# Setting a row of ones earlier and putting five zero matmuls ahead of it, in a fused RWKV-6 and SwiGLU kernel

## The chip, the cores and the metric

The kernel runs on one core of a Trainium2 chip. The core has four compute engines that run unsynchronized: TensorE (PE in the profile; its weight loads are listed as PEld), VectorE (DVE), ScalarE (ACT) and GpSimd (POOL). SyncE (SP) issues most of the transfers. The metric is the device time of one execution in microseconds; several runs are given by their median.

## The reference

Two layers follow each other. The first is a linear recurrence per batch and head with a decaying state, and u is a bonus weight for the current position:

```python
batch, n_heads, seq, head_dim = (4, 8, 768, 48)
for t in range(S):
    cur = einsum('bhd,bhe->bhde', u[None] * kt, vt)
    y[:, :, t] = einsum('bhd,bhde->bhe', rt, state + cur)
    state = wt[:, :, :, None] * state + einsum('bhd,bhe->bhde', kt, vt)
```

Its result, as 3072 rows of 384, goes through a normalization by the root mean square and a gated feed-forward layer of width 1536, whose three weight matrices are w_gate, w_val and w_out:

```python
rms = np.sqrt(np.mean(x * x, axis=-1, keepdims=True) + 1e-06)
xn = x / rms * rms_g
g = xn @ w_gate
return (g * sigmoid(g) * (xn @ w_val)) @ w_out
```

All inputs and the output are float32. The kernel computes most products in bfloat16.

## The kernel before, in words

The sequence is cut into six blocks of 128 positions (n from 0 to 5), and each block has four batches (j from 0 to 3). A tile (n, j) holds 128 positions in the partitions and 8 heads x 48 = 384 columns. For each tile the recurrence is put in its chunked form: the logarithm of w (ln, on ScalarE), its cumulative sums by matmuls with triangular masks (cs_mm), their exponentials (exp_r, exp_k), the products with r and k (r_mul and k_mul), transposes of these (rk_pe on TensorE and rk_tr, a copy out of PSUM), the scores (q_mm), their masking, the new state (st_mm, st_new) and the output (y_mm, x_add). The bonus term r * u * k is done apart: bonus_mul on GpSimd multiplies r by k and then by u_bc, bonus_sum adds up on VectorE, bonus_v multiplies by v. Then come the normalization and the feed-forward part (gate_mm, val_mm, silu, h_mul, o_mm), which take most of TensorE's time.

Every engine takes its instructions in order, and the order is written out by hand: the text ORDER lists all steps as name.n.j, and the loop at the end of the kernel issues them one by one. Transfers of r, k, v and w are issued by SyncE in that order, and it begins with load_r.0.0, load_w.0.0, u_mm.0.0, ln.0.0, load_v.0.0, load_k.0.0 and cs_mm.0.0:2.

A number behind a colon in ORDER asks for zero matmuls ahead of a step's own. They are issued in psum() (L238 and L240), when the step takes its PSUM bank: each multiplies the 128 x 128 tile zero by itself, three times side by side, 384 columns wide, into the bank that the step is about to use, with start and stop set. Their results are overwritten. The list before has such numbers at many steps up to some 38 us, the first of them the 2 of cs_mm.0.0. PSUM has three rings of banks: a and b with two banks each, and q with four (u, v, x, z).

Ahead of the steps stand the constants. VectorE sets zero first (L293), then small columns, the padding of lw and rk, and the state st (L327). GpSimd makes the identity (masks.py:197 and 199), the masks mask_lt (L297, L298) and mask_nle (L303, L304), the mask mw of the first two blocks' cumulative sums (L330 to L335), and then the row of ones (L338) and a small copy (L340).

The row of ones serves one purpose: u arrives as a single row of 384 numbers in the first partition of u_bc, and u_mm (L372) spreads it over the 128 partitions as a float32 matmul of ones_row with that row, into bank u of ring q. u_out (L375, VectorE) copies the result into u_bc, where bonus_mul (L466) reads it. The row u and the gain of the normalization are fetched by two small transfers that ScalarE issues (L288, L289).

Of the kernel before, what the change touches and what calls it, by code (L numbers as in the profile page):

```python
# [9 lines left out]
FP32 = mybir.dt.float32  # L10
# [12 lines left out]


ORDER = """
load_r.0.0 load_w.0.0 u_mm.0.0 ln.0.0 load_v.0.0 load_k.0.0 cs_mm.0.0:2 load_r.1.0 load_w.0.1 u_out.0.0 load_k.1.0
load_k.0.1 load_w.0.3 load_v.0.1 exp_r.0.0 exp_k.0.0 r_mul.0.0 cast_v.0.0 load_r.0.1 bonus_mul.0.0 load_k.1.1
bonus_sum.0.0 bonus_v.0.0 k_mul.0.0 cs_mm.1.0 load_r.1.1 load_v.1.1 load_v.1.0 load_w.0.2 rk_pe.0.0:2 rk_tr.0.0
exp_r.1.0 w_tot.1.0 w_tot.0.0 st_mm.0.0 r_mul.1.0 st_new.0.0 q_mm.0.0:4 load_k.0.3 load_r.0.3 load_r.0.2 load_k.0.2
# [100 lines left out]
def kernel(  # L130
# [13 lines left out]
    nc = tc.nc  # L144
# [16 lines left out]
    const = ctx.enter_context(tc.tile_pool(name="const", bufs=1))  # L161
# [131 lines left out]
    nc.vector.memset(zero, 0.0)  # L293
    ident = const.tile([128, 128], BF16)
    make_identity(nc, ident)
    mask_lt = const.tile([128, 128], BF16)
    nc.gpsimd.memset(mask_lt, 0.0)  # L297
    nc.gpsimd.affine_select(  # L298
# [35 lines left out]
    )  # L334
    nc.gpsimd.memset(mw[0:PD, 1], 0.0)  # L335

    ones_row = const.tile([1, 128], FP32)
    nc.gpsimd.memset(ones_row, 1.0)  # L338
    i3 = small.tile([KC, KC], FP32)
    nc.gpsimd.tensor_copy(out=i3, in_=ident[0:KC, 0:KC])  # L340
    wo_sb = persist.tile([128, FC, DM], BF16)
# [372 lines left out]
```

## Time and profile before

| | us |
|---|---|
| median of three runs | 205.89 |
| lowest and highest of them | 205.2 and 206.86 |
| the profiled execution, its own time | 203.96 |
| its span, from the first to the last instruction | 202.2 |
| TensorE busy with matmuls in it | 191.3 |
| VectorE, ScalarE and GpSimd busy | 157.5, 135.0 and 124.4 |

The profile is of one execution. A line of its timeline gives the start and the duration in microseconds, the engine, the line of the kernel, the operation, the tile written and the tiles read, their shapes, and how many alike were merged in one row; a bracket gives the idle time of the engine ahead of it and what ended that. The duration of a merged row reaches from the first start to the last end. Matmuls overlap, so their pace is read from the distance between starts. A row of the table by stage gives for each engine the busy time and, in brackets, how many instructions ran.

### The profile page before, as it was taken

How to read it: one execution, taken by the hardware profiler on the slowest of the kernel's cores; microseconds unless marked ns; L12 is line 12 of the kernel's file. 1: busy time of each engine (PE TensorE's matmuls, PEld its weight loads, DVE VectorE, ACT ScalarE, POOL GpSimd, SP SyncE). 2: the span in 40 equal slices, each digit the busy share in tenths (PEclk: the TensorE clock that was granted, in tenths of full speed). 3: DMA queues.
4: the chain of work that ended last, by engine and by line, in shares of the span. 5: the costliest groups of instructions: out<-in, count | busy, mean ns of one | idle time of the engine just before them, and what ended most of it. 6: DMA issues, size and time to landing. Idle time of an engine off the chain costs nothing.

```text
span 202.2 us, 4604 instructions
## 1 busy us (share of the span) xinstructions
PE 191.3 (95%) x1677; PEld 121.9 (60%) x1694; DVE 157.5 (78%) x307; ACT 135.0 (67%) x278; POOL 124.4 (62%) x178
## 2 busy tenths in 40 slices
PE   1999799999999999999999998999999999999993
PEld 0566485565568998865556664656555555555562
DVE  6489789799989799997999998988989782225711
ACT  2637885779699657898678985899676683335310
POOL 6488959175769962689858556988699554200000
PEclk9999999999999999999999999999999999999999
DMA  6999999999999998989899999995464013030132
GB/s 144 231 234 207 212 208 202 195 179 208 206 184 225 160 212 191 210 185 188 199 176 215 237 188 203 183 190 108 134 179 104 0 23 99 0 117 0 63 115 99
DMA packets 121567, 32.42 MB, mean 160 GB/s; under 512 B 116420, under 2 KB 120392, under 8 KB 121544
## 3 DMA queue, kind: packets, MB, share of 16 engines
q1 hardware_dynamic: 119504, 28.58, 66.6%
q0 software_dynamic: 2032, 3.54, 9.9%
q8 instruction: 13, 0.21, 0.4%
q14 instruction: 10, 0.08, 0.1%
q10 hardware_dynamic: 8, 0.00, 0.0%
HBM read 25.96 MB, written 4.72 MB: 152 GB/s over the span
## 4 chain that ended last, share of the span: by engine, by line
PE 65%; ACT 3%; DMA 2%; DVE 2%; issue 1%; SPq 0%; DVEq 0%; ACTq 0%
PE ps_av L617 7%; PE ps_bu L617 7%; PE ps_au L617 7%; PE ps_bv L617 6%; PE ps_qx L660 6%; PE ps_qv L660 6%; PE ps_qu L660 5%; PE ps_qz L660 4%; PE ps_au L622 2%; PE ps_bu L622 2%; DMA rkT<-rk 2%; PE ps_av L622 2%; PE ps_bv L622 2%; ACT L249 1%; PE ps_au L419 1%; PE ps_qv L500 1%
## 5 line engine op out<-in xcount | busy, mean ns | idle before, releaser
L660 PEld LDWEIGHTS <-ht 128*128 128x128 bf16 x300 | 28.1, 98 | 17.5 <-DVE ht L646 1.0
L251 ACT ACTIVATE sg<-ps_av 128x512 bf16<-128x512 f32 x36 | 21.5, 597 | 22.8 <-PE ps_av L617 18.0
L646 DVE TENSOR_TENSOR ht<-ps_bv,sg 128x512 bf16<-128x512 f32 x29 | 19.9, 687 | 13.9 <-PE ps_bv L617 12.9
L251 ACT ACTIVATE sg<-ps_au 128x512 bf16<-128x512 f32 x36 | 21.5, 596 | 11.5 <-PE ps_au L617 7.7
L617 PEld LDWEIGHTS <-wg_sb 128*128 128x128 bf16 x180 | 19.2, 114 | 15.9 <-issue 0.6
L617 PEld LDWEIGHTS <-wv_sb 128*128 128x128 bf16 x180 | 19.2, 114 | 15.7 <-issue 0.5
L465 POOL TENSOR_TENSOR ruk<-rt,kt 128x384 f32<-128x384 f32 x24 | 24.0, 1001 | 3.7 <-DMA kt<-in_k_dram 2.8
L475 POOL TENSOR_TENSOR ydiag<-vt,diag 128x384 f32<-128x384 f32 x24 | 20.4, 859 | 9.4 <-DVE diag L470 9.1
L617 PE MATMUL ps_av<-xnt,wg_sb 128*128 128x512 bf16 x88 | 25.0, 381 | 0.3
L466 POOL TENSOR_TENSOR ruk<-ruk,u_bc 128x384 f32<-128x384 f32 x24 | 24.0, 1001 | 1.9
L617 PE MATMUL ps_bu<-xnt,wv_sb 128*128 128x512 bf16 x86 | 24.8, 380 | 0.4
L646 DVE TENSOR_TENSOR ht<-ps_bu,sg 128x512 bf16<-128x512 f32 x31 | 21.3, 686 | 4.8 <-PE ps_bu L617 3.1
L617 PE MATMUL ps_au<-xnt,wg_sb 128*128 128x512 bf16 x87 | 23.6, 380 | 0.1
L617 PE MATMUL ps_bv<-xnt,wv_sb 128*128 128x512 bf16 x82 | 23.2, 380 | 0.2
L459 POOL TENSOR_TENSOR rk<-kt,ek 128x384 bf16<-128x384 f32 x16 | 15.9, 1001 | 9.7 <-ACT ek L251 5.9
L249 ACT ACT_TABLE_LOAD x14 | 18.0, 1283 | 1.9 <-PEq L698 1.6
L660 PE MATMUL ps_qx<-wo_sb,ht 128*128 128x384 bf16 x96 | 17.1, 326 | 0.2 <-DVE ht L646 0.2
L558 ACT ACTIVATE junk<-xb 128x384 bf16<-128x384 f32 x24 | 12.5, 522 | 6.3 <-DVE xb L553 6.2
L571 ACT ACTIVATE xn<-xb,rstd 128x384 bf16<-128x384 f32 x24 | 14.2, 609 | 0.6 <-POOL rstd L567 0.5
L470 DVE TENSOR_REDUCE diag<-ruk 128x8 f32<-128x384 f32 x24 | 13.1, 544 | 1.9 <-POOL ruk L466 1.9
L660 PE MATMUL ps_qv<-wo_sb,ht 128*128 128x384 bf16 (+1 forms) x84 | 13.8, 314 | 0.0
L251 ACT ACTIVATE lw<-wt 128x384 bf16<-128x384 f32 (+1 forms) x20 | 11.6, 583 | 2.8 <-DMA wt<-in_w_dram 2.7
(170 smaller groups left out, 408.2 us busy)
## 6 DMA issues: line engine op xcount, KB each, us to landing
rt<-in_r_dram SPq DMA_DIRECT2D x24, 192.0 KB, 4.0
vt<-in_v_dram SPq DMA_DIRECT2D x24, 192.0 KB, 3.9
kt<-in_k_dram SPq DMA_DIRECT2D x24, 192.0 KB, 3.9
out_dram<-ob SPq DMA_DIRECT2D x23, 192.0 KB, 2.2
wt<-in_w_dram SPq DMA_DIRECT2D x16, 192.0 KB, 3.7
wt<-in_w_dram SPq DMA_DIRECT2D x4, 384.0 KB, 4.3
wo_sb<-in_moe_w_out_dram POOLq DMA_DIRECT2D x3, 384.0 KB, 7.3
wg_sb<-in_moe_w_gate_dram POOLq DMA_DIRECT2D x1, 768.0 KB, 9.2
```

The costliest lines, as they stand in the source:

```text
L249: nc.scalar.preload_act_table_set(table_name)
L251: return nc.scalar.activation(**kw).ins
L459: eng.tensor_tensor(out=rk[:, n % 2, j, 1, :, 0:D], in0=inp["k", n, j], in1=bank["cs_k", n, j][:, 0:DM].rearrange("p (h d) -> p h d", h=H) ...
L465: nc.gpsimd.tensor_tensor(out=ruk[n, j], in0=inp["r", n, j], in1=inp["k", n, j], op=ALU.mult)
L466: nc.gpsimd.tensor_tensor(out=ruk[n, j], in0=ruk[n, j], in1=u_bc, op=ALU.mult)
L470: nc.vector.tensor_reduce(out=diag[n, j].rearrange("p h o -> p (h o)"), in_=ruk[n, j], axis=mybir.AxisListType.X, op=ALU.add)
L475: nc.gpsimd.tensor_tensor(out=ydiag[n, j], in0=inp["v", n, j], in1=diag[n, j].to_broadcast([128, H, D]), op=ALU.mult)
L571: nc.scalar.activation(out=xn, in_=xb[n, j], func=AF.Copy, scale=rstd[n, j][:, 1:2])
L617: nc.tensor.matmul(ps, lhsT=units(ws, c, f), rhs=x[:, c, :], start=(c == 0), stop=(c == KC - 1))
L622: nc.tensor.matmul(ps[:, i * TS // 2:(i + 1) * TS // 2], lhsT=units(ws, c, f + i), rhs=x[:, c, cols], start=(i == 0 and c == 0), stop=(i = ...
L646: nc.vector.tensor_tensor(out=ht[n][:, f, :], in0=v, in1=sg, op=ALU.mult)
L660: nc.tensor.matmul(ps[:, cols], lhsT=ht[n][:, f, b * L:(b + 1) * L], rhs=wo_sb[:, f, cols], start=(f == 0), stop=(f == FC - 1))
```

## The change

The memset of ones_row moves up on GpSimd from behind mw to directly behind the identity, ahead of both masks. In ORDER, u_mm.0.0 becomes u_mm.0.0:5, so five zero matmuls of 384 columns go into u's bank ahead of u's own. Nothing else in the order of any engine changes: VectorE, ScalarE and SyncE issue the same instructions in the same order, and the PSUM banks are the same. On TensorE the five zero matmuls and their five weight loads are its first work; the row of u's matmul follows, and behind it the two zero matmuls of cs_mm.0.0 as before.

```diff
 ORDER = """
-load_r.0.0 load_w.0.0 u_mm.0.0 ln.0.0 load_v.0.0 load_k.0.0 cs_mm.0.0:2 load_r.1.0 load_w.0.1 u_out.0.0 load_k.1.0
+load_r.0.0 load_w.0.0 u_mm.0.0:5 ln.0.0 load_v.0.0 load_k.0.0 cs_mm.0.0:2 load_r.1.0 load_w.0.1 u_out.0.0 load_k.1.0
...
     ident = const.tile([128, 128], BF16)
     make_identity(nc, ident)
+    ones_row = const.tile([1, 128], FP32)
+    nc.gpsimd.memset(ones_row, 1.0)
     mask_lt = const.tile([128, 128], BF16)
...
     nc.gpsimd.memset(mw[0:PD, 1], 0.0)
 
-    ones_row = const.tile([1, 128], FP32)
-    nc.gpsimd.memset(ones_row, 1.0)
     i3 = small.tile([KC, KC], FP32)
```

## The prediction

> **What bounds the kernel now.** I read the busy times first, then the chain of waits, then the opening fifteen microseconds engine by engine, because everything that the change touches ends before the first real matmul at 6.35 us.
>
> ```profile
> span 202.2 us, 4604 instructions
> PE 191.3 (95%) x1677; PEld 121.9 (60%) x1694; DVE 157.5 (78%) x307; ACT 135.0 (67%) x278; POOL 124.4 (62%) x178
> ...
> PE 65%; ACT 3%; DMA 2%; DVE 2%; issue 1%; SPq 0%; DVEq 0%; ACTq 0%
> ```
>
> TensorE is busy for 95% of the span, and it carries nearly all of the chain that ended last. What TensorE loses at the start is therefore lost for good, if the later stages have no slack to take it up. A table by stage tells where it loses:
>
> ```profile
> core 0: us, PE busy (x) PEld busy (x) DVE busy (x) ACT busy (x) POOL busy (x), PEclk, DMA share, GB/s
> 0.00:4.16 4.16, 0.00 (x0) 0.00 (x0) 2.62 (x10) 1.28 (x1) 3.22 (x15) 1.00 0.50 115
> 4.16:6.35 2.19, 2.19 (x5) 0.77 (x5) 0.94 (x2) 0.84 (x1) 0.09 (x1) 1.00 1.12 238
> 6.35:10.20 3.85, 3.85 (x34) 2.48 (x33) 1.61 (x4) 2.38 (x5) 2.37 (x3) 1.00 1.08 238
> 10.20:14.10 3.90, 3.44 (x48) 2.21 (x48) 3.16 (x9) 1.49 (x4) 3.40 (x4) 1.00 1.14 250
> 14.10:24.70 10.60, 9.27 (x122) 6.20 (x123) 9.38 (x19) 7.57 (x18) 9.27 (x12) 1.00 1.09 207
> 24.70:34.00 9.30, 9.25 (x107) 6.44 (x109) 8.09 (x19) 6.09 (x14) 7.12 (x9) 1.00 1.16 205
> ```
>
> TensorE idles for 4.16 us, is then busy without a break to 10.20, loses 0.46 us and 1.33 us in the next two stages, and has next to no gap after 24.7. The transfers run at their full share from 4.16 on. So the opening is a race between the loads and the first head of the chain, and TensorE's matmuls there run at half pace, as these rows of its timeline (start, duration, operation, count) show:
>
> ```profile
> 4.16 1.64 PE L372 MATMUL ps_qu<-u_bc,ones_row 1*128 1x384 f32 x2 [4.16 <-POOL ones_row L338]
> 5.74 0.82 PE L240 MATMUL ps_au<-zero 128*128 128x384 bf16 x2
> 6.35 0.85 PE L404 MATMUL ps_au<-lw,mw 128*128 128x384 bf16 x2
> 6.99 0.40 PE L408 MATMUL ps_au<-mw,lw 128*128 128x1 bf16 x8
> ...
> 9.34 0.84 PE L238 MATMUL ps_qv<-ident,zero 128*128 128x128 bf16 x6
> 9.98 0.70 PE L482 MATMUL ps_qv<-ident,rk 128*128 128x128 bf16 x8
> 10.52 0.33 PE L528 MATMUL ps_qx<-vb,rk 128*128 128x96 bf16 x4
> 10.69 0.81 PE L240 MATMUL ps_qz<-zero 128*128 128x384 bf16 x4
> ...
> 12.34 0.48 PE L411 MATMUL ps_bu<-lw,mw 128*128 128x384 bf16 x2
> 12.66 0.61 PE L482 MATMUL ps_qv<-ident,rk 128*128 128x128 bf16 x8
> ```
>
> Two 384-column matmuls take 6.99 - 6.35 = 0.64 us, 0.32 us each, at the start, and 12.66 - 12.34 = 0.32 us, 0.16 us each, later. Six 128-column transposes from 9.34 take 0.64 us, 107 ns each; the next eight take 10.52 - 9.98 = 0.54 us, which is two at 107 ns and six at about 54 ns. So the clock doubles at about 9.98 + 2 x 0.107 = 10.2 us, which is 6.0 us after TensorE's first matmul. (The PEclk column says 1.00 from the start; it does not know the state before its first record, so I go by the spacing.)
>
> **The change part by part.** First, the row of ones. It moves on GpSimd ahead of the two masks and mw. It depends on nothing but GpSimd's order:
>
> ```profile
> 1.07 0.29 POOL masks.py:199 TENSOR_SCALAR_AFFINE_SELECT ident<-ident 128x128 bf16<-128x128 bf16 x1
> 1.31 0.20 POOL L297 MEMSET mask_lt<- 128x128 bf16 x1
> ...
> 3.66 0.31 POOL L335 MEMSET mw<- 64x260 bf16 x1
> 3.91 0.20 POOL L338 MEMSET ones_row<- 1x128 f32 x1
> ```
>
> It would start where mask_lt starts, at 1.31, and be done at about 1.51 instead of 4.11. The masks and mw each come 0.20 us later, mw at about 3.97 + 0.20 = 4.17; no DMA is issued between them, and SP's and ScalarE's queues keep their order. The cover: mw is first needed by the matmul at 6.35, so there are over 1.8 us in hand. Cost nothing.
>
> Second, the row u itself. Its transfer is issued by ScalarE and moves 1.5 KB; the two packets of its queue between 1.6 and 1.8 us are the row and its completion mark:
>
> ```profile
> DMA packets 2, 0.00 MB, mean 8 GB/s; under 512 B 1, under 2 KB 2, under 8 KB 2
> q10 hardware_dynamic: 2, 0.00, 2.2%
> ```
>
> So u is there by 1.8 us, and the only thing that held u's matmul until 4.16 was the row of ones.
>
> Third, the five zero matmuls. They need only the zero tile, and they stand ahead of u's matmul on TensorE:
>
> ```profile
> 0.88 0.11 DVE L293 MEMSET zero<- 128x64 uint32 x1 [0.88 <-PEq L698]
> ```
>
> With the 0.05 us that passed between the end of the memset of ones (4.11) and the matmul behind it (4.16), they start at about 0.99 + 0.05 = 1.05 (rounded) and take 5 x 0.32 = 1.60 us, to 2.65. By then ones and u are there. u's matmul takes 5.74 - 4.16 = 1.58 us, to 4.23, and the two zero matmuls that were there before take 6.35 - 5.74 = 0.61 us, to 4.84. Then TensorE waits, for the next matmul needs ScalarE's logarithm:
>
> ```profile
> 5.42 0.84 ACT L251 ACTIVATE lw<-wt 128x768 bf16<-128x768 f32 x1 [2.50 <-DMA wt<-in_w_dram]
> 7.42 0.48 ACT L251 ACTIVATE ps_au<-ps_au 128x388 f32<-128x388 f32 x1 [1.16 <-PE ps_au L408]
> ```
>
> The logarithm waits for w's load, which nothing in the change hastens, and ends at 6.26. With an estimated 0.07 us for the hand-over (a little over the 0.05 us between GpSimd's memset and the matmul behind it) the first real matmul starts at 6.33 instead of 6.35. So u's matmul 1.5 us earlier buys 0.02 us: when it stood late it was just not late enough to hold anything. A new hole of 6.33 - 4.84 = 1.49 us stands where TensorE was busy.
>
> u's broadcast is ready earlier too. Its copy waits on VectorE behind the memset of st, and is done near 5.2 instead of 6.4. Who needs it:
>
> ```profile
> 3.25 1.34 DVE L327 MEMSET st<- 128x1536 uint32 x1 [0.27 <-issue]
> 5.84 0.56 DVE L375 COPY u_bc<-ps_qu 128x384 f32<-128x384 f32 x1 [1.25 <-PE ps_qu L372]
> 7.08 1.00 POOL L465 TENSOR_TENSOR ruk<-rt,kt 128x384 f32<-128x384 f32 x1 [2.84 <-DMA kt<-in_k_dram]
> 8.16 1.00 POOL L466 TENSOR_TENSOR ruk<-ruk,u_bc 128x384 f32<-128x384 f32 x1
> 7.93 0.56 DVE L453 TENSOR_TENSOR rk<-rt,ps_au 128x384 bf16<-128x384 f32 x1 [1.54 <-ACT ps_au L251]
> 9.19 0.55 DVE L470 TENSOR_REDUCE diag<-ruk 128x8 f32<-128x384 f32 x1 [0.70 <-POOL ruk L466]
> 9.66 0.54 DVE L459 TENSOR_TENSOR rk<-kt,ps_bu 128x384 bf16<-128x384 f32 x1
> 10.72 0.69 DVE L489 COPY rkT<-ps_qv 128x1024 bf16<-128x1024 bf16 x1 [0.52 <-PE ps_qv L482]
> ```
>
> GpSimd reads u_bc at 8.16, behind its product at 7.08, which waits for k's load. So that gain is worth nothing either.
>
> Fourth, the clock. This is where the change can act, and these same rows price it. If TensorE ran at full pace from 6.33, the cumulative sums of the first head would come earlier by half of 1.0 us; but VectorE takes the k product in order, behind the sum that waits for GpSimd, which waited for k's load: 7.08 + 1.00 + 0.08 + 1.00 = 9.16, then 9.19, then 9.66 to 10.20. The four transposes that need it start after 10.20 whatever the clock was before, and by then the clock is at full pace in this execution. What is left is the start of the copy at 10.72, which could come 0.03 us earlier. The bounds: the stretch from 6.35 to 10.2 holds 3.85 us of matmul at half pace, so an earlier clock can be worth at most half, 1.92 us, and at least nothing. I take 0.03, since the rows show the wait that hides the rest.
>
> The sum is 0.00 + 0.02 + 0.03, about 0.05 us less than the profiled execution. That execution took 203.96 us (span 202.2 and 1.8 around it), 1.93 us less than the median of 205.89 of the three runs, which themselves spread from 205.2 to 206.86. So the forecast on the scale of the median is 205.89 - 0.05, 205.8 us: no change that a measurement can tell. About 1%, 2.06 us, is what a measurement of this kernel can tell from none.
>
> [...]
>
> **The rivals.** A, faster: the clock rises early and something that I take as hidden is not. For it: counting the same 6.0 us of work from 1.05, hole included or not, puts the rise at 7.1 to 8.5 us. Against it: GpSimd's chain to 9.16. Its price goes to the bound above, 203.96 - 1.92 = 202.0 in this execution, 204.0 on the median. It would pass 1% only where executions without a profile rise later than 10.2 now.
>
> B, slower: the hole of 1.49 us undoes the first stretch, and the count of 6.0 us starts anew at 6.33, so that the clock rises at 12.3. For it: before, TensorE has no hole at all between 4.16 and the rise, so nothing in this trace shows a rise behind a broken stretch. Against it: a hole of 0.46 us ahead of 14.05 and the 1.33 us of idle time between 14.10 and 24.70 did not slow the matmuls again. The price: between 10.2 and 12.3 four transposes take 0.05 us more each, and the four zero matmuls at 10.69 take 0.32 instead of 0.16 each: 0.20 + 0.64 = 0.84 us, all ahead of the next head's sums and of VectorE's copy behind them, which waited for TensorE before:
>
> ```profile
> 13.30 0.69 DVE L489 COPY rkT<-ps_qv 128x1024 bf16<-128x1024 bf16 x1 [0.22 <-PE ps_qv L482]
> ```
>
> That gives 206.7. It decides once the rise is later than about 10.7, where the zero matmuls begin; it passes 1% once the clock stays low to about 15 us (2 x 2.06 behind 10.7, and the 0.46 us gap used up), and at 17 us it would give 205.9 + (17 - 10.7) / 2 - 0.46 = 208.6.
>
> [...]
>
> C: the change doesn't do what it says, because the zero matmuls do not count for the clock or TensorE starts late. Then the rise stays at 10.2, and 205.9 results; by the profile this differs from the forecast in the trace only, not in the time.
>
> **How the numbers follow.** The forecast with C, where the rise comes anywhere up to about 11 us and costs or brings under 0.3 us, has 0.52. A has 0.18, of which 0.08 beyond 1%. B has 0.22, of which 0.11 beyond 1%. What I have not named, the spread of runs included, has 0.08, half on each side. So faster has 0.12, slower 0.15 and the same 0.73. The range runs from 204.2, near A's bound, to 207.8, past B at 12.3 and short of its far end; some 0.09 lies below it and 0.11 above.
>
> **What would show it.** In the profile of the changed kernel: five zero matmuls at 1.05 to 2.65, u's matmul at 2.65 released by nothing late, a hole from 4.84 to 6.33 with the logarithm's end as its releaser, the first sum at 6.33, the k product on VectorE still at 9.66 and the copy at 10.72. The spacing of the transposes and zero matmuls between 9 and 13 us tells where the clock rose. I am wrong if VectorE's copies at 10.72 and 13.30 move by more than 0.3 us either way, or if w's and k's loads land at other times.

## The result and the profile after

The changed kernel is slower by half a percent: 206.08 us, median of 22 runs (204.81 to 207.55), against 205.06 us for the kernel before (median of 22, 203.73 to 206.86). The ratio is 1.0048, with a 95% interval from 1.0025 to 1.0070. The forecast was no visible change, 205.8. The profiled execution took 205.05 us (span 203.3), 1.1 us more than that of before. Single executions of either kernel spread over more than the difference, so one pair of profiles can't tell why. A ratio here leaves out executions more than 1.5% above the fastest of their kernel, and two of the profiles below, those of the kernels that the last table calls fill behind and tiny zeros, are of such executions.

The opening came out as worked out. TensorE's timeline of the changed kernel (start, duration, operation, count, and in the bracket the idle time and what ended it):

```profile
1.04 1.78 PE L240 MATMUL ps_qu<-zero 128*128 128x384 bf16 x5 [1.04 <-DVE half_of L311]
2.75 1.64 PE L372 MATMUL ps_qu<-u_bc,ones_row 1*128 1x384 f32 x2
4.33 0.82 PE L240 MATMUL ps_au<-zero 128*128 128x384 bf16 x2
6.13 0.80 PE L404 MATMUL ps_au<-lw,mw 128*128 128x384 bf16 x2 [0.98 <-ACT lw L251]
...
9.71 1.15 PE L482 MATMUL ps_qv<-ident,rk 128*128 128x128 bf16 x8
...
10.98 1.14 PE L240 MATMUL ps_qz<-zero 128*128 128x384 bf16 x4
12.05 0.23 PE L500 MATMUL ps_qz<-rkT 48*128 48x128 bf16 x1
```

The zeros, u's matmul and the hole that the logarithm ends are where the prediction has them; the bracket counts the hole from the end of the last zero matmul and gives 0.98 us. The first sum starts at 6.13, earlier than 6.33, because w's load let the logarithm begin 0.18 us earlier in this execution (5.24 against 5.42). The transposes at 9.71 are all at half pace (eight in 0.94 us, up to the next start at 10.65; eight from 13.24 take 0.44 us), and the trace's clock record begins at 11.63 us. So the clock rose 1.5 us later than in the profile before, which is rival B in a mild form. VectorE's rows answer to those of before:

```profile
9.65 0.54 DVE L459 TENSOR_TENSOR rk<-kt,ps_bu 128x384 bf16<-128x384 f32 x1
10.90 0.69 DVE L489 COPY rkT<-ps_qv 128x1024 bf16<-128x1024 bf16 x1 [0.70 <-PE ps_qv L482]
13.88 0.69 DVE L489 COPY rkT<-ps_qv 128x1024 bf16<-128x1024 bf16 x1 [0.62 <-PE ps_qv L482]
```

The k product is at 9.65 (9.66 before), and the copies are 0.18 and 0.58 us later. But what an opening loses need not last. To see what does, I set the n-th copy, sum or elementwise operation of VectorE beside the same one of the kernel before, whose order is the same. The table gives how much later it starts (us), at the time that it had before:

| profile of | clock rose | 14.6 | 21.2 | 91.2 | 109.1 | 148.6 | 152.6 | 199.0 |
|---|---|---|---|---|---|---|---|---|
| the change | 11.63 | +0.52 | +0.58 | +0.58 | +0.48 | +0.39 | +1.18 | +1.03 |
| the change, second profile | 9.57 | -0.10 | -0.50 | +0.24 | +0.85 | +0.93 | +1.87 | +1.72 |

The second profile comes from an experiment below. Its opening is faster than that of before, and it is still slower in the end. What both have in common is a jump of 0.8 to 0.9 us between 148.6 and 152.6, far from anything that the change touches. TensorE's timeline of the changed kernel has it there:

```profile
150.78 0.81 PE L617 MATMUL ps_au<-xnt,wg_sb 128*128 128x512 bf16 x3
152.30 0.23 PE L500 MATMUL ps_qz<-rkT 48*128 48x128 bf16 x1 [0.71 <-DMA rkT<-rk]
```

In the profile before, the same matmul follows with a much shorter wait:

```profile
150.39 0.81 PE L617 MATMUL ps_au<-xnt,wg_sb 128*128 128x512 bf16 x3
151.13 0.23 PE L500 MATMUL ps_qz<-rkT 48*128 48x128 bf16 x1
```

These scores need two transposed tiles of the last block, which SyncE transposes by DMA (line 487) at 147.2 and 148.6 us. The answer for that line gives the time from issue to landing, for the four transposes between 146.4 and 156 us. After:

```profile
DMA to landing us min/median/max: 2.7/3.2/4.2
```

and before:

```profile
DMA to landing us min/median/max: 2.7/2.8/2.8
```

What delayed them is seen in the transfers of the changed kernel between 148.0 and 152.4 us, in 40 slices of 0.11 us:

```profile
DMA  9612999997000100001079999999999993000000
GB/s 321 140 14 58 375 275 272 256 81 2 0 0 0 9 7 9 9 9 12 9 149 293 296 293 246 277 279 289 282 289 275 277 224 56 9 0 0 0 0 0
q1 hardware_dynamic: 2162, 0.58, 94.3%
q8 instruction: 1, 0.02, 1.3%
```

From 149.0 to 150.2 hardly anything moves. As this stop begins, one packet of another queue is under way: 16 KB on queue q8, kind "instruction", which starts at 148.52 and takes 0.93 us. There are 13 such packets of 16 KB in either profile. TensorE has 1677 matmuls and 1694 weight loads on the page of before, 259 for each packet, and the packets follow TensorE's progress through the whole span: between two of them it starts 142 to 308 such instructions before the change, 133 to 290 after it. I take it from this that the queue fetches TensorE's code.

Where in the transposes the stop falls is told by the packets of SyncE's queue (count, MB, and the time that they took as a share of 16 engines). First the changed kernel from 148.3 to 149.0, from 149.0 to 150.2 and from 150.2 to 152.0 us, and then, for a first transpose that is not disturbed, the kernel before from 147.6 to 149.0:

```profile
q1 hardware_dynamic: 505, 0.13, 309.4%
...
q1 hardware_dynamic: 28, 0.01, 5.5%
...
q1 hardware_dynamic: 1581, 0.39, 96.7%
```

```profile
q1 hardware_dynamic: 1066, 0.26, 83.9%
```

One transpose is 1024 packets of 256 bytes, 0.26 MB. So the stop falls in the middle of the first transpose, when half of it has moved, and both land late: 4.2 and 3.7 us after their issue, in place of 2.8 and 2.8. The share of 309% comes from packets that had begun when the stop came: 19 of them, started between 148.83 and 148.99, took 1.27 to 1.42 us each, where 18 ns is usual. During the stop 28 small packets pass at some 9 GB/s, and from 150.2 on the rest moves at some 290. That the packet of code holds the others up is read from the two coming together, here and in the profiles below; how it does so, the trace does not tell.

In the profile before, the packet of code starts at 150.71, when the two transposes have just landed, and the gap between them is short:

```profile
DMA  9999999200189999999600005000000000000000
GB/s 296 296 291 293 279 293 226 45 0 0 40 200 293 284 296 289 289 296 270 122 7 0 0 0 149 0 0 0 0 0 0 0 0 0 0 0 0 0 0 0
```

So the theory of the fetch is: ten more TensorE instructions move the fetch of a later block of code ahead by some 2 us (150.71 to 148.52 in these two profiles), into the transposes for which TensorE waits. The first experiments were made without it. They weigh three other theories: the hole (the clock counts anew behind it), the zeros themselves, and the added instructions as such.

### The profile page after: what moved, and what is told of

Read it like the earlier page. It is cut to its first block, busy times and chain, and to the rows that moved or that the text cites. A ratio compares the mean times of both kernels' runs of the same rounds, so it can differ in the third digit from the quotient of the medians.

```text
span 203.3 us, 4631 instructions
## 1 busy us (share of the span) xinstructions
PE 194.7 (96%) x1699; PEld 122.8 (60%) x1699; DVE 157.3 (77%) x307; ACT 135.1 (66%) x278; POOL 124.3 (61%) x178
## 4 chain that ended last, share of the span: by engine, by line
PE 58%; ACT 5%; DMA 4%; POOL 2%; DVE 1%; SPq 1%; issue 0%; DVEq 0%; ACTq 0%
PE ps_av L617 7%; PE ps_au L617 7%; PE ps_bu L617 6%; PE ps_bv L617 6%; PE ps_qu L660 5%; PE ps_qx L660 4%; PE ps_qz L660 4%; PE ps_qv L660 4%; DMA rkT<-rk 4%; PE ps_au L622 2%; PE ps_bu L622 2%; ACT L249 2%; PE ps_av L622 2%; PE ps_bv L622 2%; ACT sg L251 1%; POOL rk L459 1%
## 5 line engine op out<-in xcount | busy, mean ns | idle before, releaser
L617 PEld LDWEIGHTS <-wv_sb 128*128 128x128 bf16 x180 | 19.2, 114 | 15.7 <-issue 0.5
```

Source lines behind the costliest of these rows:

```text
L617: nc.tensor.matmul(ps, lhsT=units(ws, c, f), rhs=x[:, c, :], start=(c == 0), stop=(c == KC - 1))
```

## The experiments

**Half of the change at a time.** First the row of ones early, without the zero matmuls:

```diff
-... u_mm.0.0:5 ...   (of the change)
+... u_mm.0.0 ...
```

> The row of ones early, no zero matmuls ahead of u's. TensorE should run u's matmul from about 1.8 to 3.4 us and its two zero matmuls to 4.0, and then have a hole of some 2.2 us before the first sum. [...] Theory of the zeros (the five zero matmuls themselves cost): the time of the kernel before within 0.2%.

Measured: ratio 0.9985 (0.9949 to 1.0021), median 204.91 us. The hole is there, 1.3 us in which TensorE waits for the logarithm. The clock rose at 12.31 us, later than in either profile of the change, and yet the time is that of before. The theory of the hole, by which this kernel should lose as the change does, is wrong as an account of the loss.

Then the zero matmuls without the early row:

```diff
-... u_mm.0.0 ...   (of the kernel before)
+... u_mm.0.0:5 ...
```

> The five zero matmuls, but the row of ones where it was. Zero matmuls from 1.05 to 2.65 us, a hole to 4.16, and from there on what the kernel before does. [...] Theory of the zeros: 0.3 to 0.7% slower, as with the whole change.

Measured: 1.0031 (0.9997 to 1.0066), median 205.89. The clock rose at 8.70, and VectorE was 0.33 us early at 21 us. It lost 1.03 us between 148.6 and 152.6, so by this profile the loss goes with the zeros and not with the opening's speed.

**Closing the hole**, behind u's matmul and ahead of it:

```diff
-... cs_mm.0.0:2 ...   (of the change)
+... cs_mm.0.0:6 ...
```

> The whole change, and four more zero matmuls behind u's (six instead of two), which close the hole between 4.9 and 6.2 us. [...] Theory of the zeros: at least as slow as the change, 0.4% or more.

```diff
-... u_mm.0.0:5 ...   (of the change)
+... u_mm.0.0:9 ...
```

> The whole change with nine zero matmuls ahead of u's instead of five: zeros from 1.05 to 3.9 us, u's matmul to 5.5, two zeros to 6.1, and a hole of 0.2 us. Theory of the hole: the time of the kernel before within 0.2%. [...] Theory of the zeros: 0.5% slower or more.

Measured: 1.0017 (0.9977 to 1.0056) and 1.0015 (0.9974 to 1.0055), with medians of 206.09 and 205.97 us against 205.09 for the kernel before on the same chip. By the ratios alone these two say little: their intervals hold both no loss and the loss of the change. In the profiles the clock rose at 8.64 and 10.45, and the jump at 150 us is there in both, 0.88 and 1.13 us.

**Work or instructions.** The five zero matmuls cut to one column each:

```diff
     def u_mm(n, j):
+        ahead[at[0]] = 0
         ps = bank["u", n, j] = psum("q", ("u", n, j), [128, DM])
+        for _ in range(5):
+            nc.tensor.matmul(ps[:, 0:1], lhsT=zero, rhs=zero[:, 0:1], start=True, stop=True)
```

> The change, with the five zero matmuls ahead of u's cut to one column each: the same number of TensorE instructions, but hardly any TensorE time ahead of 2 us. Theory of early work (TensorE's being busy from 1 us is what costs): the time of the kernel before within 0.2%, near 205.2 us. Theory of the added instructions (ten more instructions ahead of all others, wherever they move the instruction stream, cost): 0.3 to 0.5% slower, near 206.0. Theory of the hole: also slower, since the hole before the first sum stays, but the run without zero matmuls has already spoken against it.

Measured: 1.0043 (1.0006 to 1.0081), median 206.28. With hardly any work ahead of u's matmul the loss stays, so early work on TensorE is not what costs.

```diff
-... u_mm.0.0:5 ... cs_mm.0.0:2 ...   (of the change)
+... u_mm.0.0 ... cs_mm.0.0:7 ...
```

> The change, with its five zero matmuls moved behind u's matmul: u's from about 1.8 or 2.4 us, then seven zeros to about 6 us, nearly no hole. Theory of early work: at most a part of the loss remains, since TensorE starts 0.8 to 1.4 us later, 205.2 to 205.7 us. Theory of the added instructions: as slow as the change, near 206.0. Theory of the hole: the time of the kernel before.

Measured: 1.0005 (0.9966 to 1.0043), median 205.98 against 205.50. The ratio can't separate the theories; the profile has the jump at 150 us, 1.16 us. This kernel and the two above close the hole or nearly so, and all three ratios lie below the 1.0048 of the change though their jumps are as large. Whether a closed hole wins something back is not shown, since all three intervals reach above 1.004.

> The change itself once more, beside the others on this chip, and for a second profile. If its loss is one of the mean and not of one set of executions: 0.2 to 0.7% slower than the kernel before. If the loss shown before came of the spread of the executions (203.4 to 207.9 us for the kernel before): within 0.2%. In its profile, if the loads decide and not TensorE's opening: the largest shifts against the kernel before stand behind waits for a load's landing, at places that differ from the first profile of the same kernel.

Measured: 1.0043 (1.0008 to 1.0078), median 206.01. The loss repeats, and this run gave the second profile in the table above.

```diff
-... u_mm.0.0:5 ... cs_mm.0.0:2 ...   (of the change)
+... u_mm.0.0 ... cs_mm.0.0 ...
```

> The row of ones early, and no zero matmuls ahead of the first sums, neither the five nor the two that were there before. The hole ahead of the first sum grows to about 2.5 us. Theory of early work and theory of the added instructions: as fast as the kernel before or up to 0.2% faster. [...]

Measured: 1.0009 (0.9977 to 1.0042), clock risen at 11.68 us, no jump at 150 us (0.01). Four instructions fewer than before do no harm and no measurable good.

**The place of the fetch.** By now every profile with ten or eighteen more TensorE instructions had the jump, and no other had it. Three kernels test the fetch itself. The first leaves the opening alone and adds the instructions later:

```diff
     def y_mm(n, j):
         ps = bank["y", n, j] = psum("q", ("y", n, j), [128, DM])
+        if (n, j) == (0, 1):
+            for _ in range(5):
+                nc.tensor.matmul(ps[:, 0:1], lhsT=zero, rhs=zero[:, 0:1], start=True, stop=True)
```

> The kernel before, its opening untouched, with five zero matmuls of one column (and their five weight loads) added at about 23 us, ahead of eight zeros that are there already and of a wait. Theory of the fetch (ten more TensorE instructions ahead of 150 us bring the fetch of TensorE's next 16 KB of instructions forward, from 150.7 us to about 148, into the transposing transfers of the last block, which TensorE then waits for): in the profile the two transposes land some 1 us later and TensorE's wait for them at about 151 us grows from 0.4 to over 1 us; the time is 0.3 to 0.6% longer. Theory that something in the opening costs (the zeros, the hole, the clock): the time of the kernel before within 0.2%, and no shift at 150 us.

Measured: 1.0063 (1.0026 to 1.0100), median 206.79. The opening of before, with ten instructions at 23 us, is as slow as the change. Its transfers, busy time by half microsecond (the last two columns are the DMA share and GB/s):

```profile
151.00:151.50 0.50, 0.50 (x5) 0.30 (x4) 0.50 (x2) 0.29 (x1) 0.50 (x2) 1.00 3.64 125
151.50:152.00 0.50, 0.50 (x5) 0.29 (x3) 0.35 (x2) 0.50 (x3) 0.50 (x1) 1.00 0.01 2
152.00:152.50 0.50, 0.50 (x4) 0.26 (x3) 0.50 (x2) 0.50 (x3) 0.50 (x2) 1.00 0.08 12
152.50:153.00 0.50, 0.45 (x3) 0.27 (x3) 0.50 (x2) 0.50 (x2) 0.50 (x1) 1.00 1.04 232
```

Again the traffic stops for about a microsecond while the two transposes are under way (issued at 149.5 and 150.8, with the fetch started at 150.73), after about half of the first. The jump in this profile is smaller, 0.42 us, and the wait for the transposes is 0.8 us, under the 1 us that I expected. The ratio stands for a larger loss, at least 0.0026 x 205 = 0.53 us by its interval, so the jump of this one profile does not account for all of it.

The second has the whole change, and takes as many instructions out again further on:

```diff
-... y_mm.0.1:8 ...   (of the change)
+... y_mm.0.1:3 ...
```

> The whole change, with five of the eight zero matmuls at about 23 us taken out, so that TensorE's instructions from there on stand where they stood before. Theory of the fetch: no shift at 150 us, the fetch at about 150.5, and the time of the kernel before within 0.2%, though the opening is that of the change. Theory that something in the opening costs: 0.3 to 0.6% slower.

Measured: 0.9981 (0.9944 to 1.0018), median 205.34 against 205.45. The opening is that of the change, with its hole and a clock that rose at 11.39, and the loss is gone. Its transfers between 148.0 and 152.4:

```profile
DMA  9999996000699999999160000000000000000000
GB/s 277 293 298 296 272 284 117 7 0 9 154 282 284 291 296 293 286 286 185 19 149 0 0 0 0 0 0 0 0 0 0 0 0 0 0 0 0 0 0 0
q8 instruction: 1, 0.02, 1.6%
```

The fetch (the lone 149 GB/s, at 150.25) comes behind the packets of both transposes, as before. The control takes the same zeros out of the kernel before:

```diff
-... y_mm.0.1:8 ...   (of the kernel before)
+... y_mm.0.1:3 ...
```

> The kernel before with the same five zero matmuls at 23 us taken out and nothing added: ten TensorE instructions fewer. It is the control of the compensated kernel, and moves the fetch the other way, to about 152 us. Theory of the fetch: behind the two transposes that TensorE waits for first, so no shift there; the time of the kernel before within 0.2%, unless it now meets the next two transposes, which would show as a later landing of these. Theory that something in the opening costs: the time of the kernel before.

Measured: 0.9991 (0.9953 to 1.0028), median 205.90 against 205.45, no jump at 150 us. Taking the zeros out is not by itself what made the compensated kernel fast. The fetch did not go later as expected; it starts 3.9 us after the issue of the first transpose, against 4.1 in the kernel before.

**More instructions, another place.** Fifteen zero matmuls of the kernel before are split into three narrow ones each, so sixty TensorE instructions are added and hardly any work:

```diff
+            elif key in (("y", 0, 1), ("qe", 1, 1)):
+                for c in range(3):
+                    nc.tensor.matmul(flat[:, c * 128:(c + 1) * 128], lhsT=zero, rhs=zero, start=True, stop=True)
```

> The kernel before, its opening untouched, with fifteen of its zero matmuls of 384 columns (the eight at 23 us and the seven of q_mm.1.1) each split into three of 128 columns: the same TensorE time, but sixty TensorE instructions more. Theory of the fetch, by its place and not by the number of instructions: the fetch moves forward by sixty instructions, some 30 matmuls, from 150.7 us to about 145 to 146, ahead of the last block's transposes, which begin to move at 148. They should land in 2.8 us again, TensorE's wait at 151 us stays at 0.4 us or less, and the time is that of the kernel before within 0.3%, though six times as many instructions are added as in the change; another of the thirteen fetches may now meet transposes elsewhere and would show as a late landing there. Theory that added instructions cost as such: 0.5% slower or more.

Measured: 1.0046 (1.0012 to 1.0080), median 205.93 against 204.90. The fetch went to 144.92 us, the two transposes landed in 2.8 us, and there is no jump at 150 (-0.05): these expectations held. The time did not: the fetch met other transfers. Between 142.1 and 145.4 us of the old time this profile loses 0.93 us. VectorE waits for an output store, a transpose of the normalized rows (line 583 here) lands in up to 4.0 us, and the transfers between 142 and 150 us, in slices of 0.2 us, have a slow tail from 146.4 to 147.8, behind the code packet (144.92 to 146.51):

```profile
147.96 0.56 DVE L670 COPY ob<-ps_qv 128x384 f32<-128x384 f32 x1 [0.85 <-DMA out_dram<-ob]
...
DMA to landing us min/median/max: 3.0/3.5/4.0
```

```profile
GB/s 48 0 0 0 28 259 200 46 1 0 200 415 338 246 458 315 16 175 251 35 0 0 8 8 15 15 18 18 11 0 0 175 273 44 1 0 54 392 422 384
q8 instruction: 1, 0.02, 1.2%
```

In the profile before, the same copy follows the instruction ahead of it at once:

```profile
145.44 0.55 DVE L667 COPY ob<-ps_qv 128x384 f32<-128x384 f32 x1
```

By the time alone, this run would also fit the theory that instructions cost as such, about 0.5% for sixty as for ten. The compensated kernel can't decide between this theory and the place of the fetch, since its count is that of the kernel before. The profile of split zeros speaks for the place: no loss at 150 us, where the fetch has left, and a loss where it has gone.

**All profiles side by side.** The second column counts the TensorE instructions added ahead of 148 us; the third is the start of the fetch, from the issue of the first transpose of the last block; the fourth is the longest time to landing of the four transposes; the last is VectorE's jump between 148.6 and 152.6 us of the old time.

| kernel | added | fetch | landing | jump |
|---|---|---|---|---|
| before | 0 | +4.1 | 2.8 | 0 |
| ones only | 0 | +3.9 | 2.8 | 0.00 |
| no zeros | -4 | +3.8 | 2.8 | 0.01 |
| compensated | 0 | +3.7 | 2.8 | 0.00 |
| fewer late | -10 | +3.9 | 2.8 | -0.01 |
| the change | +10 | +1.3 | 4.2 | 0.79 |
| the change again | +10 | +2.5 | 4.9 | 0.94 |
| zeros only | +10 | +1.3 | 4.8 | 1.03 |
| tiny zeros | +10 | +2.5 | 5.0 | 1.03 |
| zeros behind | +10 | +1.2 | 4.9 | 1.16 |
| fill behind | +18 | +1.8 | 4.9 | 0.88 |
| fill ahead | +18 | +1.3 | 4.8 | 1.13 |
| late tiny | +10 | +1.2 | 4.2 | 0.42 |
| split zeros | +60 | -4.5 | 2.8 | -0.05 |

With the fetch between 1.2 and 2.5 us behind the first issue, all eight profiles have a late landing and a jump; outside of that, none of the six has. In all eight, 18 to 29 packets of the last block's first two transposes took 1.3 to 2.1 us each; in the six, none of them took over 18 ns.

The stop is not new with the change. The kernel before has one at an earlier fetch, which starts at 65.80 us and meets transposes as well (the last columns are again the DMA share and GB/s):

```profile
65.80:66.30 0.50, 0.50 (x7) 0.50 (x6) 0.50 (x2) 0.39 (x1) 0.50 (x1) 1.00 4.23 243
66.30:67.30 1.00, 1.00 (x12) 1.00 (x10) 1.00 (x3) 1.00 (x3) 1.00 (x2) 1.00 0.57 12
67.30:67.80 0.50, 0.50 (x6) 0.44 (x5) 0.39 (x1) 0.11 (x1) 0.50 (x2) 1.00 0.22 41
```

The transposes there land in 4.3 to 5.0 us, and by the profile no engine waits for them. In split zeros that fetch starts at 63.84, no stop follows, the transposes land in 2.8 to 3.0 us, and VectorE gains nothing by it: it is 0.99 us late at 58 us of the old time and 1.00 at 74. The fetch of the kernel before at 28.82 us meets no transpose, and the traffic goes on behind it:

```profile
29.30:30.30 1.00, 1.00 (x10) 0.59 (x8) 0.70 (x2) 0.98 (x3) 0.30 (x1) 1.00 1.19 215
```

So a fetch that meets transposes costs time where something waits for these. One thing in the table's column of the fetch I can't explain: from -10 to 0 added instructions the fetch stays at 3.7 to 4.1 us, and at +10 and +18 it is at 1.2 to 2.5. It does not move in step with the count.

## Why the prediction was wrong

**The step that failed** is the one that costed the five zero matmuls: by their 1.60 us of TensorE time in an idle stretch, and by nothing else. It counted their work and the queues of SyncE, ScalarE and GpSimd, and left out the queue that, by its packets, brings TensorE's own instructions. That queue stands on the page of the profile before, 13 packets and 0.21 MB, with 0.4% of the engines' time; the prediction says nothing of where in time they fall, or of what waits there. In place of 0 for the instructions the profiles show 0.79 and 0.94 us in two executions of the change, of which 0.15 us is won back by 199 us, and the comparison gives 206.08 - 205.06 = 1.02 us. That 206.08 lies so near the forecast of 205.8 is chance: the forecast was set 0.05 us under the 205.89 of three runs, and the median of the kernel before over 22 runs is 205.06.

In the eight profiles with a late landing it was the transposes beside the fetch that TensorE waited for: at about 150 us its weight load waits 0.8 to 1.6 us for rkT in these, and stands idle for 0.4 us in the other six.

**The opening held, by its steps.** Zeros at 1.04, u's matmul at 2.75, a hole from 5.15 to 6.13, the k product at 9.65: the predicted 1.05, 2.65, 4.84 to 6.33 and 9.66 are close to that. That an earlier u and a different clock are worth next to nothing agrees with the compensated kernel, 0.9981 (0.9944 to 1.0018), within that interval. One reading was wrong without effect: the prediction has the row u there by 1.8 us. In the kernel with the ones alone, u's matmul waits for that row until 2.45:

```profile
2.45 1.61 PE L372 MATMUL ps_qu<-u_bc,ones_row 1*128 1x384 f32 x2 [2.45 <-DMA u_bc<-in_u_dram]
```

In the changed kernel the zeros, which run to 2.75, cover this.

**The clock.** I gave 0.84 us for a rise at 12.3 us, at VectorE's copy behind the second head. The kernel with the ones alone had its rise at 12.31 and was 0.80 us late at 14.6 us. So B's price was about right, and B's end was wrong: at 21.2 us that kernel was 0.04 us early. The changed kernel gave one of the prediction's own signs of being wrong, VectorE's second copy at 13.88 in place of 13.30, but its second profile lacks that shift (-0.04) and ends later still. At about 19 us GpSimd waits for v's load, which sets the pace again. The row of before, and of the changed kernel:

```profile
19.11 0.50 POOL L389 CAST vb<-vt 128x384 bf16<-128x384 f32 x1 [0.62 <-DMA vt<-in_v_dram]
```

```profile
19.61 0.90 POOL L389 CAST vb<-vt 128x384 bf16<-128x384 f32 x1 [1.00 <-DMA vt<-in_v_dram]
```

The prediction said that the opening is a race between loads and the first head, but took what TensorE loses there as lost for good; up to 20 us the loads decide. Over the fourteen profiles the shift at 21.2 us goes from -0.50 to +0.76 and does not follow the rise of the clock (rise at 7.81: +0.76; at 9.57: -0.50; at 12.31: -0.04). Similar steps of up to 2.6 us stand later, mostly around 105 us, again at a load of v, in kernels with and without added instructions. They are large enough to make the spread of the executions, which one or two profiles of a kernel can't show.

**The rivals.** A did not come: where the clock rose at 7.81, 8.64 and 8.70, the shift at 21.2 us was +0.76, +0.37 and -0.33. B came in part, as said, without being the loss. C, that the zeros do not bring the clock up, fits the two profiles of the change, with rises at 11.63 and 9.57 us against 10.16 before; its time, 205.9, lacked the fetch. The cause of the loss was in none of the three; it fell under the 0.08 for what was not named. A sum in B is off, with no effect here: by its own terms, (15.7 - 10.7) / 2 - 0.46 = 2.04, the 1% would be passed at about 15.7 us and not at 15.

On the clock, the 6.0 us that the prediction counts from TensorE's first matmul to the rise are those of one profile (4.16 to 10.16), and others do not repeat them. In the changed kernel it is 10.59 us (1.04 to 11.63), in the one with the ones alone 9.86 (2.45 to 12.31), and in zeros behind, which has next to no hole, 5.49 (2.32 to 7.81):

```profile
2.32 1.61 PE L372 MATMUL ps_qu<-u_bc,ones_row 1*128 1x384 f32 x2 [2.32 <-DMA u_bc<-in_u_dram]
3.87 2.42 PE L240 MATMUL ps_au<-zero 128*128 128x384 bf16 x7
6.08 0.84 PE L404 MATMUL ps_au<-lw,mw 128*128 128x384 bf16 x2
```

From the first sum behind the hole to the rise it is 5.50 us in the changed kernel (6.13 to 11.63) and 5.39 in the compensated one (6.00 to 11.39), near the 6.0 that B counts anew. Fill behind and fill ahead, in which TensorE does not wait for the logarithm, rose at 8.64 and 10.45, and two executions of the change itself at 11.63 and 9.57. Which of TensorE's work brings the clock up, the zeros or u's one-row float32 matmul, is not shown, and the chances that the prediction gives to A and B were my estimates.

## What to carry to other kernels

Instructions added to TensorE early moved the fetch of its later code here (from 4.1 us behind the issue of a transpose to between 1.2 and 2.5 us, with ten or eighteen); where DMA transposes stand on the path, look up when the packets of the "instruction" queues fall, and what waits for the transfers beside them. If a small edit at one place shifts the time by half a percent, set the same instructions of both traces side by side over the whole span before explaining it by the place of the edit: the loss here was 140 us away. A control that keeps the edit and restores the instruction count separates the two.

## What the runs showed of the hardware that was not expected

Where one packet of 16 KB of TensorE's code met DMA transposes, some 256-byte packets of these, which otherwise take 18 ns, took 1.3 to 2.1 us, and the traffic of the core fell to about 10 GB/s for one to two microseconds. It cost time at two places: at the rkT transposes for which TensorE waits (0.42 to 1.16 us), and at an output store and the xn transposes (0.93 us). At 66 us of the kernel before it cost none. How the one packet holds up the others, why the loss of late tiny is larger than its jump, and why the fetch jumps by some 2 us between 0 and 10 added instructions, stay open. No kernel here beats the one before clear of the intervals.
